# A banded-attention and SMELU kernel: third batch's q and k transposed by DMA instead of TensorE, and SMELU of eight early slots back on VectorE

## The chip, the cores and the metric

The kernel runs on one core of one Trainium2 chip. The metric is the device time of one execution in microseconds, the median of several runs.

## The reference

Eight batches of eight heads of attention over 576 tokens, head size 64, in which a token sees only tokens at most 32 away. The result is laid out as 4608 rows of 512 and goes through two matrix products with SMELU between them.

```python
B, H, S, D = q.shape                      # 8, 8, 576, 64
scores = np.matmul(q, k.transpose(0, 1, 3, 2)) / np.sqrt(D)
pos = np.arange(S)
scores = np.where(np.abs(pos[:, None] - pos[None, :]) <= 32, scores, -1e9)
attn = softmax(scores)                    # exp(s - max) / sum
x = np.matmul(attn, v).transpose(0, 2, 1, 3).reshape(B * S, H * D)      # 4608 x 512
h = x @ w_in                              # w_in 512 x 2048
g = np.where(h >= 1, h, np.where(h <= -1, 0, (h + 1) ** 2 / 4))         # SMELU
out = g @ w_out                           # w_out 2048 x 512
```

Inputs and output are float32; the kernel works in bfloat16 on TensorE, with float32 sums in PSUM.

## The kernel before, in words

Every engine's instructions stand in the order in which the code writes them; nothing reorders them, so an instruction that waits holds all behind it on its engine.

**The slots.** After a start that does the first half of batch 0's attention, the main loop runs over slots `a`. Tokens are worked in 18 tiles of 256, and each tile takes 8 slots, one for each 256 columns of `w_in`: `t, f = divmod(a, 8)`. A slot issues on TensorE the "hp block", 8 matmuls of 128x256 (L489) into a PSUM tile `hp`. ScalarE then makes `rr = relu(h/2 + 1/2)` (L493). VectorE makes the SMELU from it in two passes: `mx = max(h, rr)` (L500) and `g = min(rr, 1) * mx` (L501), into `gT[t]`. For the eight slots in `two_on_act` ScalarE makes a second pass instead, `mx = rr^2` (L497), and VectorE only one, `g = min(max(h, 1), mx)` (L498). `hp` has two buffers in the pool `ps_h` (slots 6 and 7 use the pool `ps_o`), so the hp block of slot n+2 waits until VectorE has read `hp` of slot n.

**The second product** follows in pieces. For the first two token tiles a piece is `pair(x)` (L445, 8 matmuls of 128x256), placed in slots by the list `pairs`. From then on it is `quarter(x)` (L429, 4 matmuls of 128x512), one a slot, 8 slots behind. `pair(3)` and `pair(7)` complete the first two output pieces: ScalarE copies them (L450) and SyncE (SP) sends them out (L451).

**Attention** is hung into the slots by the table `ev`. `scores` (L227) multiplies q by k for two heads' pairs and ScalarE takes exp (L235) into `pt`. The band mask is added on TensorE ahead of the scores by `add_mask` (L206) in slots below 14, and multiplied by VectorE afterwards (L201, with `mask4` and `mask8`) from slot 14 on. `sums` (L293) multiplies the weights with v and with ones; ScalarE makes the reciprocal by Ln and Exp (L299, L300), and VectorE writes the normalized rows into `xT` (L305, L308), at the next call of `flush()`. Scores and sums use the one-buffer PSUM pools `ps_s` and `ps_n`. Each hp block reads 256 tokens of `xT`: the slots from 8 on need the rest of batch 0, and the slots from 16 on need the first 192 tokens of batch 1, which come from the two `sums` of slot 14.

**q and k** must stand head-dimension-first. Batches 1 and 2 (`b < LONG`, second and third) are loaded in long rows (`load_rows`, L92, 9 tokens in one run) and transposed by TensorE in `tposes` (L187, 36 matmuls for q, 36 for k), through tiles of `ps_s` and `ps_n`, and ScalarE and VectorE copy the result to `qT` and `kT` (L190). Batches from `LONG` on are loaded in natural rows (`load_nat`, L98, 64 numbers in one run) and transposed by DMA from the SP queue (`xpose`, L194). The GpSimd (POOL) queue issues all loads, in the order of the code, each of them after the eighth load before it has landed.

```python
at(14, seq[0][0], (*seq[1][0], ps_s))            # the two first sums of batch 1
for n, a in enumerate((13, 13.5, 16, 18, 20, 25, 27)):
    at(a, seq[n][1])                             # scores; slot 25: first of batch 2
for b, *a in ((1, 11, 12), (2, 19.5, 21.5)):
    for t in range(2):
        at(a[t], (tposes, b, (t, 0), (t, 1)))    # q, then k
```

A slot's order of issue is: hp block and SMELU, `flush()`, events at `a`, pairs or quarter, events at `a + 0.5`, `xpose`.

Of the kernel before, what the change touches and what calls it, by code (L numbers as in the profile page):

```python
# [9 lines left out]
AF = mybir.ActivationFunctionType  # L10
ALU = mybir.AluOpType
# [3 lines left out]
def kernel(  # L15
# [20 lines left out]
    B, H, S, D = q.shape  # L36
    NT, DM, DFF = out.shape[0], 512, 2048
# [4 lines left out]
    TAIL = S - MAIN  # L42
    RING = 4 * S
    PAD = 32
    LONG = 3

    const = ctx.enter_context(tc.tile_pool(name="const", bufs=1))
    nat = ctx.enter_context(tc.tile_pool(name="nat", bufs=2))
# [7 lines left out]
    ps_s = ctx.enter_context(tc.tile_pool(name="ps_s", bufs=1, space=bass.MemoryType.PSUM))  # L56
# [7 lines left out]
    band = const.tile([128, 192], BF, name="band")  # L64
    bias = const.tile([128, 192], BF, name="bias")
    mask4 = const.tile([128, 8 * 128], BF, name="mask4")
    mask8 = const.tile([128, 4 * TAIL], BF, name="mask8")
# [6 lines left out]
    V, P, A = nc.vector, nc.gpsimd, nc.scalar  # L74


    qn, kn, vn = {}, {}, {}
    HD = (slice(0, 64), slice(64, 128))

    def load_half(half, t, h, eng=None, x=None):  # L80

# [61 lines left out]
    def put(todo):  # L143
        for fn, *x in todo:
            fn(*x)

    w = [(load_w_in, c, c + 256, h) for c in range(0, 1024, 256) for h in range(2)]
    w += [(load_w_in, 1024, 1536, h) for h in range(2)]
    w += [(load_w_in, c, c + 256, h) for c in range(1536, DFF, 256) for h in range(2)]
    put(w[:4] + [(load_half, 1, t, h) for t in range(2) for h in range(2)] + w[4:])  # L150
    P.tensor_copy(band[HD[1], 0:128], band[HD[1], 64:192])
    for m, n, x in ((mask4, 8, 128), (mask8, 4, TAIL)):
        P.tensor_copy(m.rearrange("p (n j) -> p n j", n=n),
                      band[:, :x].rearrange("p (n j) -> p n j", n=1).to_broadcast([128, n, x]))
    put([(load_w_out, 0, n) for n in range(2)] + [(load_rows, 1, t) for t in range(2)])
    put([(load_v, 1, n) for n in range(4)] + [(load_w_out, 1, n) for n in range(2)])
    put([(load_rows, 2, t) for t in range(2)] + [(load_v, 2, n) for n in range(4)])


    kT = {}  # L160
# [1 line left out]
    def qkT(b, t):  # L162
        if t == 0:
            return qTs[b % 3][:, PAD:]
        if b not in kT:
            kT[b] = ktp.tile([128, NY * S], BF, name="kT")
        return kT[b]

    def tpose(b, n, t, copy, ps):


        half, part = divmod(n, 2)
        j0, j1 = ((0, 5), (5, 9))[part]
        if b:
            src = qn[b] if t == 0 else kn[b]
            src = [src[:, half + 2 * h] for h in range(2)]
            dst = qkT(b, t).rearrange("d (y e p j) -> d y e p j", y=2, e=2, j=9)[:, half, :, :, j0:j1]
            like = "d j (e p) -> d e p j"
        else:
            src = (qn, kn)[t][b, half]  # L180
            src = src if src.shape[1] == 9 else [src[:, h] for h in range(2)]
            dst = qkT(b, t).rearrange("d (y l p j) -> d l y p j", l=2, p=32, j=9)[:, half, :, :, j0:j1]
            like = "d j (p y) -> d y p j"
        for j in range(j0, j1):
            if isinstance(src, list):
                for h in range(2):
                    nc.tensor.transpose(ps[HD[h], j - j0], src[h][:, D * j:D * j + D], ident)  # L187
            else:
                nc.tensor.transpose(ps[:, j - j0], src[:, j], ident)
        return lambda: copy(dst, ps[:, :j1 - j0].rearrange(like, p=64 if b else 32))  # L190
# [12 lines left out]
    def add_mask(ps, n, w):  # L203
        for a in range(2):
            for h in range(2):
                nc.tensor.matmul(ps[h][HD[a], :n * w].rearrange("p (n j) -> p n j", n=n), ident[HD[h], HD[h]],  # L206
                                 bias[HD[h], 64 * h:64 * h + w].rearrange("p (n j) -> p n j", n=1)
                                 .to_broadcast([64, n, w]),
                                 start=True, stop=False, skip_group_check=True)

    def scores(b, ys, pars, cs, eng, pool=ps_s):
# [8 lines left out]
        for y1 in range(*ys):  # L220
            for par in range(*pars):
                for c2 in range(*cs):
                    c = 2 * c2 + par
                    for a in range(2):
                        for h in range(2):
                            s0 = S * (y1 + 2 * a) + 64 * c
                            nc.tensor.matmul(ps[HD[a], h, 128 * n:128 * n + 128], kT[b][HD[h], s0:s0 + 64],  # L227
                                             qTs[b % 3][HD[h], PAD + s0 - 32:PAD + s0 + 96],
                                             start=eng is not None, stop=True, skip_group_check=True)
# [81 lines left out]
    def flush():  # L311
        while muls:
            muls.pop(0)()
# [32 lines left out]
    with tc.tile_pool(name="ps_p", bufs=1, space=bass.MemoryType.PSUM) as ps_p:  # L346
        keep_warm(14, ps_h, "hp")

        V.memset(qkT(0, 0).rearrange("d (y s) -> d y s", y=NY)[:, :, S // 2:352], 0.0)
        for b in range(LONG):  # L350
            V.memset(qkT(b, 0).rearrange("d (y s) -> d y s", y=NY)[:, :, S - PAD:], 0.0)
# [23 lines left out]

    NB = NT // TB
    NF = DFF // 256
    pairs = [(8, 0), (9, 1), (10, 2), (11, 3), (12, 4), (13, 5), (15, 6), (15, 8), (16, 7), (17, 9)]
    two_on_act = (1, 2, 7, 8, 9, 10, 11, 12)
    ev = {}  # L380

    def at(a, *todo):


        ev.setdefault(a, []).extend(x for x in todo if x)

    def steps(b, cut):

        for k, (lo, hi) in enumerate(((0, cut), (cut, MAIN))):
            for y1 in range(2):  # L390
                yield (sums, b, y1, lo, hi), (scores, b, (y1, y1 + 1), (0, 2), (2 * k, 2 * k + 2))
        yield (sums, b, 0, MAIN, S), (scores8, b)
# [4 lines left out]
    at(4, (sums, 0, 1, TB, MAIN))  # L397
    at(5, (sums, 0, 0, MAIN, S, ps_s))
    seq = [x for b in range(1, B) for x in steps(b, 224)]
    at(14, seq[0][0], (*seq[1][0], ps_s))  # L400
    for n, a in enumerate((18, 20, 22, 27)):
        at(a, seq[2 + n][0])
    for n, a in enumerate((13, 13.5, 16, 18, 20, 25, 27)):
        at(a, seq[n][1])
    sl = [30, 32, 35, 39, 42, 45, 49, 52, 56, 59, 62, 65, 69, 73, 77, 81, 84, 88, 92]
    sl += [96, 99, 103, 106, 110, 113, 116, 120, 124, 128]
    for n, a in enumerate(sl):
        at(a, seq[6 + n][0], seq[7 + n][1] if n < len(sl) - 1 else None)
    for b, *a in ((1, 11, 12), (2, 19.5, 21.5)):
        for t in range(2):  # L410
            at(a[t], (tposes, b, (t, 0), (t, 1)))
    loads, xps = {}, {}
    for b in range(LONG, B):
        a = sl[5 * (b - 1) - 7] - 17
        for t in range(3):
            loads.setdefault(a + t, []).append((b, t))
        for t in range(2):
            xps.setdefault(a + 5 + t, []).append((b, t))

    gT, op = {}, {}  # L420
# [33 lines left out]
    def run(pos):  # L454
        todo = []
        for fn, *x in ev.get(pos, []):
            if fn is sums:
                todo.append(sums(*x))
            elif fn is tposes:
                tposes(*x)  # L460
            else:
                pool = (x.pop(),) if x[-1] in (ps_s, ps_n, ps_o) else ()
                fn(*x, eng, *pool)
        for end in todo:
            end()

    for a in range(NF * NB + NF):
        t, f = divmod(a, NF)
        eng = None if a < 14 else V
        post = [x for n, x in pairs if n == a] + [a - NF] * (a >= 2 * NF + 2)  # L470
        for b, x in loads.get(a, []):
            if x < 2:
                load_nat(b, x)
            else:
                for n in range(4):
                    load_v(b, n)
        if a == 0 or a > 3:
            flush()
        if t < NB:
            if t not in gT:  # L480
                gT[t] = gtp.tile([128, 2 * NF, TB], BF, name="gT", tag="gT")
            r0 = TB * t % RING
            if a in (6, 7):
                hp = ps_o.tile([128, 2, TB], FP, name="hp", tag="op")
            else:
                hp = ps_h.tile([128, 2, TB], FP, name="hp", tag="hp")
            for j in range(2):
                for n, kk in enumerate((0, 2, 1, 3)):
                    nc.tensor.matmul(hp[:, j], w_in[:, kk, 256 * f + 128 * j:256 * f + 128 * j + 128],  # L489
                                     xT[:, kk, r0:r0 + TB], start=n == 0, stop=n == 3)  # L490

            rr = ewp.tile([128, 2, TB], FP, name="rr")
            A.activation(rr, hp, AF.Relu, scale=0.5, bias=0.5)  # L493
            g = gT[t][:, 2 * f:2 * f + 2]
            mx = ewp.tile([128, 2, TB], FP, name="mx")
            if a in two_on_act:
                A.activation(mx, rr, AF.Square)  # L497
                V.scalar_tensor_tensor(g, hp, 1.0, mx, op0=ALU.max, op1=ALU.min)  # L498
            else:
                V.tensor_max(mx, hp, rr)  # L500
                V.scalar_tensor_tensor(g, rr, 1.0, mx, op0=ALU.min, op1=ALU.mult)  # L501
        flush()
        run(a)
        for x in post:
            (pair if x < 4 * 4 else quarter)(x)
        run(a + 0.5)
        for x in xps.get(a, []):
            xpose(*x)
# [30 lines left out]
```

## Time and profile before

| What | Before |
|---|---|
| median of 3 runs | 314.97 us (314.94 to 315.1) |
| the profiled execution | 315.1 us, of which the span is 313.0 us |
| TensorE (PE) busy | 304.1 us, 97% of the span |
| VectorE (DVE) busy | 243.7 us, 78% |
| ScalarE (ACT) busy | 196.2 us, 63% |
| chain that ended last | PE 90%, ACT 4%, DVE 3% |
| SMELU passes L500, L501, L498 | 689, 692, 690 ns each |
| ScalarE pass L497 | 630 ns |
| granted TensorE clock | 1.0 throughout |

The page's second part cuts the span into 40 slices of 7.8 us and gives tenths of busy time. The chain is the sequence of work followed back from the last instruction; where it leaves PE, PE was waiting. A timeline line gives start, duration, engine, source line, tiles, and in brackets how long the engine was idle before it and what released it.

### The profile page before, as it was taken

To read this page: it belongs to the slowest core of one execution; us is meant where nothing else is said; L and a number is where in the kernel's file an instruction comes from. 1 tells how busy PE (TensorE), PEld (TensorE's weight loads), DVE (VectorE), ACT (ScalarE), POOL (GpSimd) and SP (SyncE) were. 2 spreads that over 40 slices of the span, in tenths; PEclk is the share of its full clock that TensorE was granted. 3 is DMA by queue.
4 is the path that set the end of the run, shared out by engine and by line. 5 is a ranking of instruction groups with operands and counts; after the bars stand their busy time and mean duration, and the time that the engine had idled before them with its cause. 6 is when DMAs were issued, how large, how long until landed. Compare 5 with 4: busy or idle time off the path is not lost.

```text
span 313.0 us, 8615 instructions
## 1 busy us (share of the span) xinstructions
PE 304.1 (97%) x3711; PEld 207.9 (66%) x3711; DVE 243.7 (78%) x380; ACT 196.2 (63%) x324; POOL 72.3 (23%) x88
## 2 busy tenths in 40 slices
PE   8988999999999999999999999999999999999995
PEld 3566878776666666666666666666666666666652
DVE  3359558878888888888888888888888888878760
ACT  2788886866765766567666666566676666654431
POOL 8797354653051314040604000000000000000000
PEclk9999999999999999999999999999999999999999
DMA  9999999999999989896996792006501000100111
GB/s 151 183 186 198 175 207 186 179 160 163 165 176 139 111 175 159 74 110 133 166 109 69 76 154 69 34 36 112 109 36 36 37 34 36 37 36 34 48 55 67
DMA packets 124102, 34.54 MB, mean 110 GB/s; under 512 B 108192, under 2 KB 119712, under 8 KB 124064
## 3 DMA queue, kind: packets, MB, share of 16 engines
q0 software_dynamic: 94720, 18.06, 77.9%
q1 hardware_dynamic: 29200, 15.63, 21.4%
q8 instruction: 29, 0.48, 0.6%
q10 hardware_dynamic: 144, 0.29, 0.4%
q14 instruction: 9, 0.07, 0.1%
HBM read 36.70 MB, written 9.44 MB: 147 GB/s over the span
## 4 chain that ended last, share of the span: by engine, by line
PE 90%; ACT 4%; DVE 3%; issue 1%; ACTq 0%
PE hp L489 38%; PE op L429 36%; PE bb L293 6%; PE op L445 4%; PE bb L227 2%; PE z L336 2%; ACT pt L235 2%; PE tp L187 1%; DVE xT L305 1%; ACT rc L300 1%; ACT lr L299 1%; DVE kT L190 1%; DVE qT L190 1%; DVE mx L500 1%; ACT rr L493 0%
## 5 line engine op out<-in xcount | busy, mean ns | idle before, releaser
L489 PE MATMUL hp<-xT,w_in 128*128 128x256 bf16 x1152 | 149.3, 273 | 2.0 <-DVE xT L308 1.2
L493 ACT ACTIVATE rr<-hp 128x512 f32<-128x512 f32 x144 | 85.6, 595 | 87.1 <-PE hp L489 86.2
L489 PEld LDWEIGHTS <-w_in 128*128 128x128 bf16 x1152 | 112.0, 98 | 41.6 <-issue 2.6
L429 PE MATMUL op<-w_out,gT 128*128 128x512 bf16 x512 | 130.4, 380 | 0.0
L500 DVE TENSOR_TENSOR mx<-hp,rr 128x512 f32<-128x512 f32 x136 | 93.7, 689 | 33.2 <-ACT rr L493 31.3
L501 DVE SCALAR_TENSOR_TENSOR gT<-rr,mx 128x512 bf16<-128x512 f32 x136 | 94.1, 692 | 4.6
L429 PEld LDWEIGHTS <-gT 128*128 128x128 bf16 x512 | 47.5, 98 | 36.8
L235 ACT ACTIVATE pt<-bb 128x1024 bf16<-128x1024 f32 (+1 forms) x33 | 33.2, 1012 | 4.6 <-PE bb L227 3.1
L106 POOL DMA_DIRECT2D vn<-in_v_dram x32 | 27.3, 864 | 35.4 <-PE bb L227 32.3
L305 DVE TENSOR_TENSOR xT<-bb,rc 128x512 bf16<-128x512 f32 (+1 forms) x32 | 21.0, 657 | 11.0 <-ACT rc L300 10.3
L434 ACT COPY osb<-op 128x512 f32<-128x512 f32 x32 | 18.6, 583 | 11.6 <-PE op L429 11.1
L300 ACT ACTIVATE rc<-lr 128x512 f32<-128x512 f32 (+2 forms) x40 | 23.5, 587 | 1.3
L299 ACT ACTIVATE lr<-bb 128x512 f32<-128x512 f32 (+2 forms) x40 | 22.0, 550 | 0.8 <-PE bb L293 0.7
L98 POOL DMA_DIRECT2D qn<-in_q_dram x10 | 12.2, 1222 | 43.1 <-DMA qT<-qn 37.8
L293 PE MATMUL bb<-pt,ones 64*64 64x256 bf16 (+3 forms) x352 | 19.5, 255 | 1.5 <-DVE kT L190 0.8
L201 DVE TENSOR_TENSOR pt<-pt,mask 128x1024 bf16<-128x1024 bf16 (+1 forms) x33 | 20.2, 613 | 0.1
L293 PE MATMUL bb<-pt,vn 64*64 64x128 bf16 (+3 forms) x712 | 18.2, 204 | 0.0
L293 PEld LDWEIGHTS <-ones 64*64 64x64 bf16 x352 | 10.2, 105 | 9.9 <-issue 9.9
L293 PEld LDWEIGHTS <-vn 64*64 64x64 bf16 x712 | 16.7, 107 | 0.0
L445 PE MATMUL op<-w_out,gT 128*128 128x256 bf16 x128 | 16.5, 273 | 0.0
L98 POOL DMA_DIRECT2D kn<-in_k_dram x10 | 12.1, 1214 | 10.0 <-DMA kT<-kn 3.8
L227 PE MATMUL bb<-qT,kT 64*64 64x128 bf16 x520 | 13.2, 217 | 0.3 <-DVE kT L190 0.2
(56 smaller groups left out, 120.8 us busy)
## 6 DMA issues: line engine op xcount, KB each, us to landing
out_dram<-osb SPq DMA_DIRECT2D x36, 256.0 KB, 2.3
vn<-in_v_dram POOLq DMA_DIRECT2D x32, 144.0 KB, 8.9
qn<-in_q_dram POOLq DMA_DIRECT2D x10, 288.0 KB, 7.4
kn<-in_k_dram POOLq DMA_DIRECT2D x10, 288.0 KB, 8.0
w_out<-in_moe_w_out_dram POOLq DMA_DIRECT2D x4, 512.0 KB, 12.5
w_in<-in_moe_w_in_dram POOLq DMA_DIRECT2D x12, 128.0 KB, 6.4
qn<-in_q_dram POOLq DMA_DIRECT2D x2, 576.0 KB, 13.5
kn<-in_k_dram POOLq DMA_DIRECT2D x2, 576.0 KB, 14.7
```

The source lines that it names most:

```text
L98: nc.gpsimd.dma_start(out=x[:, :, h], in_=src[b, NY * h:NY * h + NY].rearrange("y s d -> (y s) d") .rearrange("(u p) d -> p u d", p=128))
L106: nc.gpsimd.dma_start(out=vn[b][64 * a:64 * a + 64, :, h], in_=v[b, y:y + 2].rearrange("y s d -> (y s) d") .rearrange("(c r) d -> r c d", ...
L235: A.activation(p, ps[:, :, :128 * n].rearrange(like, y=m), AF.Exp, scale=D ** -0.5)
L293: nc.tensor.matmul(bb[HD[h], a, o + c0:o + c1], ones[HD[a]] if c is None else vn[b][HD[a], c, h], p(a, h), start=n == 0, stop=True, skip_g ...
L299: A.activation(lr[:, :, :D0], bb[:, :, D0:2 * D0], AF.Ln)
L300: A.activation(rc[:, :, :D0], lr[:, :, :D0], AF.Exp, scale=-1.0)
L429: nc.tensor.matmul(o, gT[tt // 2][:, j, 128 * (tt % 2):128 * (tt % 2) + 128], w_out[:, j], start=not done, stop=len(done) == 2 * NF - 1, s ...
L445: nc.tensor.matmul(o[:, tt], gT[p][:, j, 128 * tt:128 * tt + 128], w_out[:, j, 256 * half:256 * half + 256], start=not done, stop=len(done ...
L489: nc.tensor.matmul(hp[:, j], w_in[:, kk, 256 * f + 128 * j:256 * f + 128 * j + 128], xT[:, kk, r0:r0 + TB], start=n == 0, stop=n == 3)
L493: A.activation(rr, hp, AF.Relu, scale=0.5, bias=0.5)
L500: V.tensor_max(mx, hp, rr)
L501: V.scalar_tensor_tensor(g, rr, 1.0, mx, op0=ALU.min, op1=ALU.mult)
```

## The change

Four things move together. Batch 2's q and k are loaded by `load_nat` and transposed by DMA (`xps` 17 and 18), so its 72 transposing matmuls and their 8 copies go. `two_on_act` goes, so all slots have one ScalarE pass and two VectorE passes. The two masks are built by four VectorE copies in slot 10, no longer by GpSimd before the loop. And the early schedule is laid out otherwise: the first pairs stand in slot 10 instead of 8 and 9, batch 1's transposes half a slot later, its second scores in slot 14.5 (so multiplied by the mask, not with the mask added on TensorE), its first sums in slot 15 instead of 14. The last half of `w_in` comes in pieces of 512 columns.

```diff
-    LONG = 3
+    LONG = 2
...
-    w += [(load_w_in, 1024, 1536, h) for h in range(2)]
-    w += [(load_w_in, c, c + 256, h) for c in range(1536, DFF, 256) for h in range(2)]
+    w += [(load_w_in, c, c + 512, h) for c in range(1024, DFF, 512) for h in range(2)]
...
-    P.tensor_copy(band[HD[1], 0:128], band[HD[1], 64:192])
-    for m, n, x in ((mask4, 8, 128), (mask8, 4, TAIL)):
-        P.tensor_copy(m.rearrange("p (n j) -> p n j", n=n),
-                      band[:, :x].rearrange("p (n j) -> p n j", n=1).to_broadcast([128, n, x]))
...
-    put([(load_rows, 2, t) for t in range(2)] + [(load_v, 2, n) for n in range(4)])
+    put([(load_nat, 2, t) for t in range(2)] + [(load_v, 2, n) for n in range(4)])
...
-    pairs = [(8, 0), (9, 1), (10, 2), (11, 3), (12, 4), (13, 5), (15, 6), (15, 8), (16, 7), (17, 9)]
-    two_on_act = (1, 2, 7, 8, 9, 10, 11, 12)
+    pairs = [(10, 0), (10, 1), (11, 2), (12, 3), (13, 4), (14, 5), (15, 6), (16, 7)]
...
-    at(14, seq[0][0], (*seq[1][0], ps_s))
+    at(15, seq[0][0], (*seq[1][0], ps_s))
...
-    for n, a in enumerate((13, 13.5, 16, 18, 20, 25, 27)):
+    for n, a in enumerate((13.5, 14.5, 16, 18, 20, 25, 27)):
...
-    for b, *a in ((1, 11, 12), (2, 19.5, 21.5)):
-        for t in range(2):
-            at(a[t], (tposes, b, (t, 0), (t, 1)))
-    loads, xps = {}, {}
-    for b in range(LONG, B):
+    for t, a in enumerate((11.5, 12.5)):
+        at(a, (tposes, 1, (t, 0), (t, 1)))
+    loads, xps = {}, {17: [(2, 0)], 18: [(2, 1)]}
+    for b in range(LONG + 1, B):
...
-        post = [x for n, x in pairs if n == a] + [a - NF] * (a >= 2 * NF + 2)
+        post = [x for n, x in pairs if n == a] + [a - NF] * (a >= 2 * NF)
...
-            if a in two_on_act:
-                A.activation(mx, rr, AF.Square)
-                V.scalar_tensor_tensor(g, hp, 1.0, mx, op0=ALU.max, op1=ALU.min)
-            else:
-                V.tensor_max(mx, hp, rr)
-                V.scalar_tensor_tensor(g, rr, 1.0, mx, op0=ALU.min, op1=ALU.mult)
+            V.tensor_max(mx, hp, rr)
+            V.scalar_tensor_tensor(gT[t][:, 2 * f:2 * f + 2], rr, 1.0, mx, op0=ALU.min, op1=ALU.mult)
         flush()
+        if a == 10:
+            for h in range(2):
+                for m, n, w in ((mask4, 8, 128), (mask8, 4, TAIL)):
+                    V.tensor_copy(m[HD[h]].rearrange("p (n j) -> p n j", n=n), band[HD[h], 64 * h:64 * h + w]
+                                  .rearrange("p (n j) -> p n j", n=1).to_broadcast([64, n, w]))
         run(a)
```

More of the change, by code (lines that the diff above doesn't have):

```diff
@@ L77 @@
     qn, kn, vn = {}, {}, {}
-    HD = (slice(0, 64), slice(64, 128))
     def load_half(half, t, h, eng=None, x=None):
@@ L167, in qkT @@
         return kT[b]
+    HD = (slice(0, 64), slice(64, 128))
     def tpose(b, n, t, copy, ps):
@@ L493 @@
             A.activation(rr, hp, AF.Relu, scale=0.5, bias=0.5)
-            g = gT[t][:, 2 * f:2 * f + 2]
             mx = ewp.tile([128, 2, TB], FP, name="mx")
-            if a in two_on_act:
-                A.activation(mx, rr, AF.Square)
-                V.scalar_tensor_tensor(g, hp, 1.0, mx, op0=ALU.max, op1=ALU.min)
-            else:
-                V.tensor_max(mx, hp, rr)
-                V.scalar_tensor_tensor(g, rr, 1.0, mx, op0=ALU.min, op1=ALU.mult)
-        flush()
+            V.tensor_max(mx, hp, rr)
+            V.scalar_tensor_tensor(gT[t][:, 2 * f:2 * f + 2], rr, 1.0, mx, op0=ALU.min, op1=ALU.mult)
+        flush()
+        if a == 10:
[3 more added lines that the diff above has]
+                                  .rearrange("p (n j) -> p n j", n=1).to_broadcast([64, n, w]))
         run(a)
```

## The prediction

> **What bounds the kernel now.** I read the page first. Its row of slices has PE at nine tenths nearly everywhere after the start, and the DMA engines full for the first third:
>
> ```profile
> PE   8988999999999999999999999999999999999995
> DVE  3359558878888888888888888888888888878760
> DMA  9999999999999989896996792006501000100111
> ```
>
> TensorE bounds the kernel: work taken off it, or idle time of it filled, is time gained. After 72 us PE does not idle, and the change alters no instruction of the later slots but where batch 2's q and k come from. So the question is at what time the hp block of slot 24 (`a` = 24) starts: 69.36 us now.
>
> Second, the chain of waits in order of time, where it leaves PE:
>
> ```profile
> 28.80 0.56 DVE xT L308
> 29.40 1.03 PE hp L489 x8
> ...
> 57.97 0.69 DVE gT L501
> 58.66 1.28 DVE qT L190 x2
> 59.94 0.04 issue
> 59.98 0.60 PE bb L293 x18
> ...
> 64.89 1.38 DVE kT L190 x2
> 66.27 0.04 issue
> 66.31 0.49 PE bb L293 x19
> ```
>
> Slot 8 waits for VectorE's last row of xT; the sums of slots 20 and 22 wait for the copies of batch 2's transposed q and k, which hold the PSUM tile that the sums need. Third, the PE timeline gives the prices around those two:
>
> ```profile
> 57.04 1.20 PE L187 MATMUL tp<-ident,qn 128*64 128x128 bf16 x36
> 58.17 1.05 PE L489 MATMUL hp<-xT,w_in 128*128 128x256 bf16 x8
> 59.98 0.30 PE L293 MATMUL bb<-pt,ones 64*64 64x256 bf16 x4 [0.76 <-DVE qT L190]
> ```
>
> Fourth, the VectorE timeline shows its pace: 0.72 us from mx to gT, 0.61 on to the next, so 1.33 a slot with two passes; a one-pass slot is 0.64.
>
> ```profile
> 28.80 0.55 DVE L308 TENSOR_TENSOR xT<-bb,rc 128x384 bf16<-128x384 f32 x1
> 29.27 0.68 DVE L500 TENSOR_TENSOR mx<-hp,rr 128x512 f32<-128x512 f32 x1
> 29.98 0.69 DVE L501 SCALAR_TENSOR_TENSOR gT<-rr,mx 128x512 bf16<-128x512 f32 x1
> 30.59 0.68 DVE L498 SCALAR_TENSOR_TENSOR gT<-hp,mx 128x512 bf16<-128x512 f32 x1
> ```
>
> PE's own pace is 0.87 for an hp block, a pair or a quarter, 0.97 for the one before half-array work.
>
> **Slots 1 and 2: two passes instead of one.** ScalarE loses a 0.63 pass that nobody then waits for. VectorE has slot 0's gT at 17.78; slot 1's two passes follow at 18.39 and 19.11, the two copies of batch 0's transposes at 19.72 and 20.36, ending at 21.09. They end at 20.60 now (begun at 19.23 and 19.87). PE's scores wait for that copy, ScalarE's exp for the scores, and ScalarE then runs without a gap up to the last reciprocal, so slot 8 starts at 29.40 + 0.49 = 29.89. **Loss 0.49.**
>
> **Slots 7 to 12 on VectorE, pairs from slot 10.** VectorE in the new order: slot 6 at 29.76, slot 7 at 31.08, slot 8's mx from 32.41 to 33.10. PE's hp blocks of slots 8 and 9 stand at 29.89 and 30.76, end at 31.63, and no pair follows. Slot 10's block needs slot 8's `hp`, so it starts at 33.13: **1.50 of PE idle.** Pairs 0 and 1 then fill PE, and its next need (slot 9's mx, 34.43) is met.
>
> **The mask copies in slot 10** stand on VectorE ahead of slot 11's SMELU and batch 1's q copies. No row shows such a copy. Nearest is L201, the same shape and type with two inputs: 0.683 for 1024 columns, 0.351 for 384, some 0.61 and 0.28 in sequence, so two of each cost 1.78. At one column per VectorE cycle (the 512-column passes, 0.69) they would cost 3.1; they cannot cost less than nothing. I take 1.78. From 36.40 they end at 38.18, slot 11's passes at 39.51, the q copies at 40.24 and 40.89. PE comes to the k transposes at 40.55 and needs the first tile there, the second at 41.1: no wait, cost nothing. At 3.1 the second copy ends at 42.2 and PE loses 1.1. The Trainium skill (VectorE: DVE Perf Modes, section "The perf-mode tier table (the rule you actually need)") rates a bf16 copy within SBUF at twice a two-input operation; that would make it an estimated 0.9, and the sum would stay as it is.
>
> **Slots 13 to 16.** PE: k transposes 40.55, slot 13 at 41.68, pair 4, first scores with their mask 43.52, slot 14 at 44.12, pair 5, second scores 45.98, slot 15 at 46.34, first sums 47.31. The mask matmuls that the second scores lose save 0.21, and the 0.32 for which PE waits ahead of them now (its pair ends at 43.26, they start at 43.58) goes. But the second scores' exp (1.02) ends at 47.45 and VectorE's mask product (0.69) at 48.17, so the second sums start at 48.19 instead of 47.74: 0.45 idle. Behind them ScalarE does Ln, Exp, Ln, Exp from 47.95, ending at 50.28 (2.34, as 45.73 to 48.07 now), and VectorE's xT ends at 50.92. Slot 16 needs it. PE is free at 49.51, after pair 6; two of each block's first matmuls read only the earlier half, so its effective start is 50.95 - 0.22 = 50.73: **1.22 idle.** In the kernel before, the sums stand a slot earlier with two pairs behind, and xT lands at 48.72 as slot 16 starts.
>
> Then pairs 7 and 8, slot 17, pair 9; slot 18 at 55.54 instead of 52.55: **2.99 behind**, made of 0.49 + 1.50 + 0.45 + 1.22, less 0.53 for the mask matmuls and their wait, and 0.14 of smaller changes of order.
>
> **Batch 2's transposes go.** Each block of 36 costs PE 1.22 (pair 11 at 56.08 + 0.87 = 56.95, next hp block 58.17), twice: 2.44. The sums behind come 1.81 and 1.82 after their hp block instead of 0.97: 1.69 more. **Gain 4.13.** What is late next is the release of the sums' tile by the xT product before: 2.93 after slot 18's scores end, at 60.33, and the sums come at 60.91. It just holds. VectorE and ScalarE lose eight copies (0.72 to 0.76 each), and nobody waits for those.
>
> **The sum:** 2.99 - 4.13 = -1.14; slot 24 at 68.22, the first scores of batch 2 at 70.9.
>
> **The loads.** Now the row loads of batch 2 land at 50.4 and 53.5 (issued 34.8 and 37.9, 15.6 to landing). Natural rows have 9 times as many runs. What these cost is in the next batch: its four pieces land from 60.5 to 67.1, 9.3 us after the v pieces before them (57.8), where the row loads took 5.9 after w_out (47.6). So q lands near 52, k near 57, and all behind 3.4 later: v at about 61 to 65 with the transposes between, needed at 75 (slot 27's sums). A rule speaks against this load: the Trainium skill (DMA: Bandwidth & Descriptors, section "Specifications") puts 512 B as the least run for full rate, and these write 128 B; were the rate halved, k would by estimate land at 59.4, and the sum stays. The w_in pieces move the same bytes; the last lands at 26.4 now and slot 6 comes at 26.8, so they stay hidden. POOL issues what follows some 3 us earlier (two issues of 0.6 and mask copies of 1.8 less), but into full DMA engines: nothing.
>
> **The DMA transposes** stand on SP behind the second output piece (pair 7, 52.05, copied by about 53.8), so q can go at 54.4. Nearest row, with POOL's loads still landing beside it:
>
> ```profile
> 79.91 5.26 SPq L194 DMA_TRANSPOSE qT<-qn  x1
> 85.34 2.64 SPq L194 DMA_TRANSPOSE kT<-kn  x1
> ```
>
> They landed 7.4 and 6.0 after issue (4.8 and 5.2 for the next batch, on quieter queues). So q lands at 61.8, k goes at 59.9 and lands at 66 to 67.5; scores want both at 70.9: hidden, with 3.4 to spare. Behind them on SP wait two output pieces, which have a third buffer, and POOL's batch-4 loads, which wait for q now too (61.06).
>
> **The rivals.** *A, as summed* (0.50): span 311.9. The profiled 315.1 has 2.1 outside the span, and its 315.1 is 0.13 above the median: 313.0 - 1.14 + 2.1 - 0.13 = 313.8. *B, a stall of mine is not there* (0.10): if slot 16's xT is in time, another 1.22 comes off, 312.6; against it speaks the 2.34 of ScalarE, which the trace shows in one piece. *C, kT of batch 2 comes late* (0.25): the four loads and v of batches 2 and 3 are in flight during these transposes, all 16 engines full, where the row above had only the last v pieces. If each takes twice as long, SP holds k until 65, k lands at 77, and PE waits 6 us: 319.9. It decides from 72.1 on; k at 74 gives 316.9. For it speaks the 5.26 against 2.77 on the quieter queue; against it that 12 us are free for what took 11.4. *D, VectorE's masks at one column a cycle* (0.15): 1.1 lost, 314.9, no change. That the change does not do what it says I rule out: the instruction orders show the transposes gone from PE and put on SP.
>
> **How the numbers follow.** A measurement can tell about 0.2%, 0.63 us. Faster by more: B and most of A, 0.55. Within: D and the weak end of A, 0.20. Slower: C, 0.25. The range runs from 312.2 (B, with 0.4 of error in A's steps) to 316.6, which takes in D and those cases of C with k before 73.7.
>
> **What would show it.** Right: slot 8 near 29.9, PE idle by 1.5 ahead of slot 10 and by 1.2 ahead of slot 16 with VectorE as releaser, no wait at the sums of slots 20 and 22, kT landed before 70. Wrong: PE waiting at slot 25's scores for a DMA (C), a k-transpose wait on qT copies (D), or slot 18 before 54.5 (B).

## The result and the profile after

The changed kernel takes 318.98 us (median of 4 runs, 318.45 to 319.5) against 315.04 (4 runs) of the kernel before: ratio 1.0125, 95% interval 1.0106 to 1.0143. It is slower by 3.9 us. The forecast was 313.8. Times told "by the ratios" further on are differences of such ratios, times 315 us.

The page's slices (7.9 us each) show where:

```profile
PE   8988898996999999999999999999999999999995
PEclk9999999997999999999999999999999999999999
DMA  9999999999999999978992963005510000000111
```

In the tenth slice, 71 to 79 us, PE is at six tenths and the granted clock at seven. DMA stays at nine tenths through the first 17 slices, where it was 14 before. The PE timeline of the changed kernel at that place:

```profile
68.08 1.04 PE L483 MATMUL hp<-xT,w_in 128*128 128x256 bf16 x8
68.96 1.03 PE L423 MATMUL op<-w_out,gT 128*128 128x512 bf16 x4
69.82 1.04 PE L483 MATMUL hp<-xT,w_in 128*128 128x256 bf16 x8
74.31 0.42 PE L223 MATMUL bb<-qT,kT 64*64 64x128 bf16 x16 [3.45 <-DMA kT<-kn]
74.66 1.47 PE L423 MATMUL op<-w_out,gT 128*128 128x512 bf16 x4
75.92 1.91 PE L483 MATMUL hp<-xT,w_in 128*128 128x256 bf16 x8
77.62 1.49 PE L423 MATMUL op<-w_out,gT 128*128 128x512 bf16 x4
78.95 1.04 PE L483 MATMUL hp<-xT,w_in 128*128 128x256 bf16 x8
...
80.30 0.40 PE L223 MATMUL bb<-qT,kT 64*64 64x128 bf16 x16
```

The same two scores in the kernel before:

```profile
72.06 0.42 PE L227 MATMUL bb<-qT,kT 64*64 64x128 bf16 x16
...
76.37 0.40 PE L227 MATMUL bb<-qT,kT 64*64 64x128 bf16 x16
```

Slot 24 starts at 68.08, 1.28 earlier than before (69.36). Then the scores of slot 25 wait for batch 2's kT until 74.31; before, they stood at 72.06. And the blocks after the wait are slow: a quarter takes 1.47 instead of 1.03, an hp block 1.91 instead of 1.04. From these scores to those of slot 27 (80.30) it takes 5.99, against 4.31 before (72.06 to 76.37). At slot 27 the kernel is 3.93 behind; at slot 39 (the first scores of batch 3) it is 4.03 behind, 104.54 against 100.51, and in the last stretch 4.05. So the account is -1.28 up to slot 24, +3.53 of waiting (from 1.28 ahead to 2.25 behind at slot 25's scores), +1.68 of slow blocks.

SP's timeline has the reason for the late kT:

```profile
54.18 7.29 SPq L190 DMA_TRANSPOSE qT<-qn  x1
61.57 6.81 SPq L190 DMA_TRANSPOSE kT<-kn  x1
```

The durations there are the times for which SP is held; the landing comes later. It stands in the view of q's transpose, and for k in the chain that ended last:

```profile
DMA to landing us min/median/max: 13.9/13.9/13.9
```

```profile
61.57 12.70 DMA kT<-kn
```

They went out when forecast (54.4), but qT landed 13.9 and kT 12.7 us after issue. Batch 3's, at 83.9 and 91.0, took 14.5 and 13.5, and kT landed just as slot 39's scores came.

### The profile page after: what moved, and what is told of

Read it like the earlier page. It is cut to its first block, busy times and chain, and to the rows that moved or that the text cites. A ratio compares the mean times of both kernels' runs of the same rounds, so it can differ in the third digit from the quotient of the medians.

```text
span 317.4 us, 8453 instructions
## 1 busy us (share of the span) xinstructions
PE 303.3 (96%) x3635; PEld 206.5 (65%) x3635; DVE 247.9 (78%) x388; ACT 189.1 (60%) x312; POOL 72.7 (23%) x85
## 4 chain that ended last, share of the span: by engine, by line
PE 75%; DMA 18%; POOL 4%; issue 1%; ACT 0%; POOLq 0%
PE op L423 36%; PE hp L483 33%; DMA kn<-in_k_dram 12%; PE bb L289 5%; DMA kT<-kn 4%; DMA qh<-in_q_dram 2%; PE bb L223 2%; POOL w_in L109 2%; POOL vn L105 1%; POOL w_out L114 1%; POOL qn L97 0%; POOL kh L84 0%; POOL qn L91 0%; ACT osb L428 0%; PE bb L248 0%
## 5 line engine op out<-in xcount | busy, mean ns | idle before, releaser
L489 DVE TENSOR_TENSOR mx<-hp,rr 128x512 f32<-128x512 f32 x144 | 99.2, 689 | 36.2 <-ACT rr L487 34.1
L490 DVE SCALAR_TENSOR_TENSOR gT<-rr,mx 128x512 bf16<-128x512 f32 x144 | 99.6, 692 | 4.9
L97 POOL DMA_DIRECT2D qn<-in_q_dram x12 | 14.6, 1219 | 52.6 <-DMA qT<-qn 46.0
L197 DVE TENSOR_TENSOR pt<-pt,mask 128x1024 bf16<-128x1024 bf16 (+1 forms) x34 | 20.9, 615 | 3.1 <-ACT pt L231 3.1
L295 ACT ACTIVATE lr<-bb 128x512 f32<-128x512 f32 (+2 forms) x40 | 22.1, 552 | 0.1
L97 POOL DMA_DIRECT2D kn<-in_k_dram x12 | 14.5, 1217 | 11.1 <-DMA kn<-in_k_dram 6.8
## 6 DMA issues: line engine op xcount, KB each, us to landing
w_out<-in_moe_w_out_dram POOLq DMA_DIRECT2D x4, 512.0 KB, 13.6
```

What stands on the lines that cost most here:

```text
L97: nc.gpsimd.dma_start(out=x[:, :, h], in_=src[b, NY * h:NY * h + NY].rearrange("y s d -> (y s) d") .rearrange("(u p) d -> p u d", p=128))
L295: A.activation(lr[:, :, :D0], bb[:, :, D0:2 * D0], AF.Ln)
L490: V.scalar_tensor_tensor(gT[t][:, 2 * f:2 * f + 2], rr, 1.0, mx, op0=ALU.min, op1=ALU.mult)
```

## The experiments

Theory: the transposes land late because POOL's loads of batch 3 (and 4) fill the same DMA engines; the wait lowers the granted clock; the early slots cost what was forecast. Rivals: a transpose takes 13 us there whatever is beside it; they start too late on SP; the early VectorE work is the loss.

**The DMA transposes alone, in the kernel before** (`x1_before_dma`).

```diff
-    LONG = 3
+    LONG = 2
...
-    put([(load_rows, 2, t) for t in range(2)] + ...
+    put([(load_nat, 2, t) for t in range(2)] + ...
...
-    for b, *a in ((1, 11, 12), (2, 19.5, 21.5)):
+    for b, *a in ((1, 11, 12),):
-    loads, xps = {}, {}
-    for b in range(LONG, B):
+    loads, xps = {}, {17: [(2, 0)], 18: [(2, 1)]}
+    for b in range(LONG + 1, B):
```

> The kernel before with one part of the change: batch 2's q and k in natural rows and transposed by DMA in slots 17 and 18; SMELU, masks, pairs and sums as before. Theory (the DMA transposes land late, because batch 3's loads fill the DMA engines): PE comes to slot 25's scores 4.1 us earlier than before, at 67.9, and waits there until kT lands at 72 to 74, then runs some us at a lower granted clock: 316 to 318, the 4.1 us of removed work all swallowed. Rival (the loss comes from the early slots' VectorE work, the transposes are hidden): 310.9.

Measured: 319.04 us against 314.61 of the kernel before beside it (ratio 1.0131, 1.0113 to 1.015). The PE timeline:

```profile
66.94 1.04 PE L489 MATMUL hp<-xT,w_in 128*128 128x256 bf16 x8
73.36 0.64 PE L227 MATMUL bb<-qT,kT 64*64 64x128 bf16 x16 [5.38 <-DMA kT<-kn]
73.93 1.89 PE L429 MATMUL op<-w_out,gT 128*128 128x512 bf16 x4
```

PE was ready at 67.9, as expected, and stood until 73.36; the slow blocks follow. The early slots are those of the kernel before, and the time is that of the changed kernel: with the loads as they are, kT's landing sets the time whatever TensorE gained. In this execution the wait ends 1.30 later than the scores stood before, and the blocks up to slot 27's scores (79.55) lose another 1.88: 3.2. The median lies 1 us above the expected range; why it is above this execution, which took 318.35, was not looked into.

**The early slots alone** (`x2_after_pe`): the changed kernel with batch 2 back on TensorE.

```diff
-    LONG = 2
+    LONG = 3
...
-    put([(load_nat, 2, t) for t in range(2)] + ...
+    put([(load_rows, 2, t) for t in range(2)] + ...
...
-    for t, a in enumerate((11.5, 12.5)):
-        at(a, (tposes, 1, (t, 0), (t, 1)))
+    for b, *a in ((1, 11.5, 12.5), (2, 19.5, 21.5)):
+        for t in range(2):
+            at(a[t], (tposes, b, (t, 0), (t, 1)))
-    loads, xps = {}, {17: [(2, 0)], 18: [(2, 1)]}
-    for b in range(LONG + 1, B):
+    loads, xps = {}, {}
+    for b in range(LONG, B):
```

> The kernel after with batch 2's q and k loaded in long rows and transposed by TensorE in slots 19 and 21 as before; the early slots as after. Theory: no wait at slot 25; only the early slots' loss of 2.99 us stays (some of it may be paid back at the sums of slots 20 and 22): 317.0 to 318.0, clock 1.0. Rival (the early slots cost all of the 4 us): 319.

Measured: 317.19 against 314.61 (1.008, 1.006 to 1.0099): 2.6 us, clock 1.0, slot 25's scores at 74.56, 2.50 late. The early slots cost nearly what the sum said (2.99), not the whole of the 3.9.

**Loads of batch 3 held back** (`x3_after_hold`): GpSimd reads 8 columns of kT before it issues them.

```diff
+    held = const.tile([128, 8], BF, name="held")
...
         for b, x in loads.get(a, []):
+            if (b, x) == (3, 0):
+                P.tensor_copy(held, qkT(2, 1)[:, 0:8])
```

> The kernel after, but GpSimd copies 8 columns of batch 2's kT ahead of batch 3's loads, so that these go out only when kT has landed. Theory (contention with batch 3's loads): qT lands 5 to 8 us after issue instead of 13.9, kT before 69, PE does not wait at slot 25 and the clock stays at 1.0: 313.5 to 314.5. Rival (a transpose of this size takes 13 us in this place whatever runs beside it): kT at 74, 318 to 319.

Measured: 314.53 against 314.61 (0.9993, 0.9981 to 1.0005), by the ratios 4.2 less than the changed kernel. SP's and PE's timelines:

```profile
54.08 6.29 SPq L191 DMA_TRANSPOSE qT<-qn  x1
60.47 3.94 SPq L191 DMA_TRANSPOSE kT<-kn  x1
```

```profile
70.69 0.42 PE L224 MATMUL bb<-qT,kT 64*64 64x128 bf16 x16
100.10 0.42 PE L224 MATMUL bb<-qT,kT 64*64 64x128 bf16 x16 [0.80 <-DMA kT<-kn]
```

Issued at the same times, q landed after 10.4 us, later than the expected 5 to 8 (some of batch 2's v still beside it), and k after 5.9, at 66.4. Slot 25 does not wait. That rules out the rival of a fixed 13 us. The held loads now meet batch 3's transposes, with batch 4's: these took 14.5 and 14.0, and slot 39 waits 0.80. The gain was less than expected by that.

**Filling the wait** (`x4_after_warm`): idle matmuls ahead of slot 25's scores.

```diff
+        if a == 25:
+            z = two_banks(ps_s)
+            for _ in range(14):
+                nc.tensor.matmul(z[:, 0], warm[:, :128], warm, start=True, stop=True)
         run(a)
```

> The kernel after with 14 idle matmuls of 128x512 (about 3.0 us at full clock) on TensorE ahead of slot 25's scores, in the time in which it waits for kT. Theory (1.7 us of the loss is the lower clock after the wait): scores still at 74.3, then full clock: 317.0 to 317.5. Rival (the slow blocks after the wait have another cause, such as DMA traffic): 318.5 to 319.5.

Measured: 317.26 against 314.61 (1.0073, 1.0046 to 1.0101).

```profile
69.90 3.18 PE L500 MATMUL bb<-warm 128*128 128x512 bf16 x14
73.31 0.42 PE L223 MATMUL bb<-qT,kT 64*64 64x128 bf16 x16 [0.23 <-DMA kT<-kn]
73.66 1.04 PE L423 MATMUL op<-w_out,gT 128*128 128x512 bf16 x4
```

This execution ran 0.8 us ahead of the changed kernel's already at slot 25's hp block (69.02 against 69.82) and issued its transposes as much earlier, so the scores came at 73.31 and not at the 74.3 expected. kT is as late as ever after its issue (12.7), but the blocks behind it run at full speed: 4.32 to slot 27's scores (77.63), as in the kernel before. So the slow blocks come from PE standing idle, not from the DMA traffic, and adding useless matmuls took some 1.6 us off the kernel (by the ratios), although slot 39's scores now wait 0.47 for batch 3's kT.

**Both holds, on both kernels** (`y1_before_dma_hold2`, `y2_after_hold2`): `x1_before_dma` and the changed kernel with

```diff
+    held = const.tile([128, 8], BF, name="held")
...
+            if b in (3, 4) and x == 0:
+                P.tensor_copy(held, qkT(b - 1, 1)[:, 0:8])
```

> The kernel before with only batch 2's q and k transposed by DMA (slots 17 and 18), and with batch 3's loads held until batch 2's kT has landed, batch 4's until batch 3's has. Theory (TensorE gains 4.1 us by the removed transposes, and only the loads beside the DMA transposes take it back): slot 25's scores at 67.9 without a wait, no wait at slot 39's scores: 310.5 to 311.5. Rival (a DMA transpose lands late whatever loads are held): waits at slot 25 or 39 and 313 or more.

> The kernel after with both holds: batch 3's loads until kT of batch 2 has landed, batch 4's until kT of batch 3 has. Theory: the 0.8 us wait at slot 39 that the single hold left goes, and what remains is the early slots' 2.9 loss against the transposes' 4.1 gain: 313.0 to 313.8. Rival (the wait at slot 39 moves on to a later batch): 314.3 to 314.7.

Measured: the first 310.63 against 314.69 (0.9876, 0.9861 to 0.9891), the second 313.5 (0.996, 0.9948 to 0.9973). TensorE waits for a DMA transpose in neither, though batch 4's, which no hold protects, still take 13.2 to 14.5 us. In the second qT and kT of batch 2 landed 7.5 and 6.3 us after issue, the row from which the forecast was made (7.4 and 6.0), and the time is the forecast's, 313.8, within 0.3. The first keeps the early slots of the kernel before and gets the whole 4.1 us; it beats both kernels.

**Both transposes earlier on SP** (`y3_after_early`).

```diff
-    loads, xps = {}, {17: [(2, 0)], 18: [(2, 1)]}
+    loads, xps = {}, {15: [(2, 0), (2, 1)]}
```

> The kernel after with both DMA transposes of batch 2 issued at the end of slot 15, ahead of the second output piece on SP's queue; no load is held. Rival theory (they land late because they stand behind that piece): qT goes at 51 and lands by 59, no wait at slot 25, 313.5 to 314.5. Theory (contention): each still takes 12 to 14 us to land, kT at 70.5 to 72, the wait shrinks to 0 to 1.5 us and the clock stays up, and batch 3's kT comes late by up to 1 us instead: 314.3 to 316.

Measured: 316.0 (314.65 to 317.7) against 314.69 (1.0038, 1.0019 to 1.0056).

```profile
51.57 7.66 SPq L190 DMA_TRANSPOSE qT<-qn  x1
59.33 6.46 SPq L190 DMA_TRANSPOSE kT<-kn  x1
```

Going 2.6 us sooner, they still took 13.6 and 13.1 to land; kT came at 72.4 and slot 25 waited 1.73, without a drop of the clock; slot 39 waited 0.83, as the theory had it. The place on SP matters only as far as it moves the landing.

**The SMELU alone** (`y4_before_smelu`): the kernel before with `two_on_act = ()`.

> The kernel before with two_on_act empty: all slots have two VectorE passes; pairs, masks, sums and transposes as before. Theory (of the early loss, the two passes alone cost only the 0.49 us of slots 1 and 2, the 1.5 us of slot 10 comes from the pairs that no longer stand in slots 8 and 9): 315.0 to 315.6. Rival (the extra VectorE passes of slots 7 to 12 cost PE the 1.5 us themselves): 316.4 to 317.0.

Measured: 314.87 against 314.69 (1.0008, 0.9999 to 1.0017), span 313.5 against 313.0. Slot 8 starts at 29.85 instead of 29.40, and slot 25's scores, 72.06 before, come 0.49 late:

```profile
29.85 1.03 PE L489 MATMUL hp<-xT,w_in 128*128 128x256 bf16 x8 [1.31 <-DVE xT L308]
...
72.55 0.42 PE L227 MATMUL bb<-qT,kT 64*64 64x128 bf16 x16
```

So with pairs in slots 8 and 9 nothing more is lost. The medians put the whole loss at 0.25 us (-0.03 to 0.53 by the interval), so it is no more than about the 0.49 forecast, and the medians alone do not tell it from nothing. The extra VectorE passes hide under the pairs; without pairs there, PE waits for them. That the rest of the early loss is the moved pairs and sums is read from the waits of the changed kernel; they were not moved back alone.

## Why the prediction was wrong

**The early slots were right.** Forecast and measured: slot 8 at 29.89 and 29.71; slot 10 at 33.13 and 32.96; slot 18 at 55.54 and 55.41; slot 24 at 68.22 and 68.08. That the times agree to 0.2 us is partly luck: `x4_after_warm`, whose code up to slot 25 is the same, has slot 8 at 28.92. The waits stood where they were put:

```profile
32.96 1.03 PE L483 MATMUL hp<-xT,w_in 128*128 128x256 bf16 x8 [1.35 <-DVE mx L489]
...
48.06 0.29 PE L289 MATMUL bb<-pt,ones 64*64 64x224 bf16 x4 [0.39 <-DVE pt L197]
...
49.93 0.38 PE L483 MATMUL hp<-xT,w_in 128*128 128x256 bf16 x2 [0.33 <-DVE xT L301]
50.81 0.81 PE L483 MATMUL hp<-xT,w_in 128*128 128x256 bf16 x6 [0.51 <-DVE xT L301]
```

The brackets count from the modelled end of the matmul before, the prediction from its pace of 0.87; counted in that way slot 10's wait is 1.51 (1.50 forecast) and slot 16's 1.17 (1.22).

The sums of slots 20 and 22 no longer wait. The mask copies, four in 1.19 us busy, were cheaper than the 1.78 taken and cost PE nothing, as said. The Trainium skill (VectorE: DVE Perf Modes, "The perf-mode tier table (the rule you actually need)") was nearer with its estimated 0.9.

**The loads were right**: batch 2's natural q landed at 51.1 (forecast 52), k at 55.2 (57). Batch 3's behind them were put 3.4 us later than before; they landed from 66.0 to 77.7 instead of 60.5 to 67.1, so they ran beside the transposes the whole time.

**The step that failed is the landing of the DMA transposes.** "So q lands at 61.8, k goes at 59.9 and lands at 66 to 67.5 ... hidden, with 3.4 to spare": they landed at 68.1 and 74.3. The price came from the nearest row, 7.4 and 6.0 us, which was taken while only the last v pieces ran beside it. Beside POOL's full queue the transposes of batches 2 and 3 land in 12.7 to 14.5 us in every run that had it so (the changed kernel, `x1_before_dma`, `x4_after_warm`, `y3_after_early`). With the next batch's loads held, k lands in 5.5 to 8.3 (batch 2 of `x3_after_hold`, batches 2 and 3 of `y1_before_dma_hold2` and `y2_after_hold2`). The q ahead of it, beside its batch's own v loads issued ahead of the hold, takes 7.5 to 13.6: what the hold makes early for certain is k. The page's DMA row could not have told the two places apart: it has nine tenths at the row's place too (80 to 91 us in the kernel before); the loads issued and not yet landed tell them apart.

The row was the right one for `y2_after_hold2` and the wrong one for this place. Rival C described exactly this and had a chance of 0.25; its own landing for a doubled price, 77, was near the 74.3: the landings nearly doubled (13.9 and 12.7 for 7.4 and 6.0), but SP was held 7.29 by q, not the doubled 10.5, so k went out at 61.6 and not at 65. The argument against it ("12 us are free for what took 11.4") compared a time under light load with a window under full load. Its 12 is not worked out either; by the prediction's own times the window is 16.5 us, from 54.4 to 70.9, and the two transposes took 20.1.

**The price of the wait was also too small.** C gave 316.9 for kT at 74; 318.98 was measured. C counted the idle time alone. In the changed kernel PE was idle for 3.45 us, and the blocks after it ran at a lower granted clock, the third figure from the end of each line (after the window's length and the busy times of PE, PEld, DVE, ACT and POOL):

```profile
74.00:76.00 2.00, 1.69 (x21) 0.81 (x22) 0.16 (x1) 1.02 (x1) 1.19 (x1) 0.78 1.43 258
76.00:78.00 2.00, 2.00 (x10) 1.29 (x9) 0.53 (x1) 0.08 (x1) 0.02 (x1) 0.50 2.43 155
```

There 1.68 us went. The waits of up to 1.73 us in these runs lowered nothing. The Trainium skill (TensorE: Matmul & The Clock Gate, Part 1) has the clock fall after at least one idle window of about 3.4 us. The runs agree only roughly: in `x1_before_dma` PE's last matmul ended at 67.98, and the clock was 0.63 on average from 70 to 72 us and 0.50 from 72 to 76. With a fall from 1.0 to 0.5 that puts it near 70.5, after 2.5 us of idle PE. What a wait between 1.73 and 2.5 us does was not measured.

## What to carry to other kernels

The price of a transfer is read from a row with the same traffic beside it: here the same transpose landed in 4.6 to 14.5 us, and the loads that filled the engines were for a batch whose q was not transposed before 83.9. Work moved off the bounding engine is won only if the new path lands by the new, earlier time of need; when it doesn't, first look for loads running far ahead of need that can be held back, before giving the path up. And count the lower clock with a long TensorE wait: up to 1.73 us it cost nothing more here, at 3.45 us it cost 1.68 more, and in one run the clock fell after 2.5 us.

## What was not expected of the hardware

- Loads and transposes slow each other: batch 3's k pieces landed 20.0 and 22.1 us after issue in the changed kernel, against 14.2 and 13.3 before and 13.8 for the second in `x2_after_pe`, where TensorE transposes batch 2. SP itself is held 6.5 to 7.7 us by a transpose of batch 2 or 3 beside the full queue, against 2.4 to 3.6 for the transposes of the kernel before from 110 us on.
- Issuing loads later made two kernels faster, by the ratios: the changed kernel by 4.2 us with the first hold and another 1.0 with the second, `x1_before_dma` by 8.0 with both.
